# An attention, expert and gated-layer kernel: gated weights prepared ahead and kept in DRAM

## The chip, the cores and the metric

The program runs on one core of a Trainium2 chip. The metric is the device time of one execution, in microseconds (us). TensorE (PE in the profile) multiplies matrices, PEld is its weight load; VectorE is DVE, ScalarE is ACT, GpSimd is POOL; all DMAs here are issued by SyncE (SP).

## The reference

Three layers follow each other. An attention over 2 batches, 8 heads, 576 positions, width 64, where half of the heads see a local window of 32 positions and half see every 32nd position. Its output, 1152 tokens of width 512, goes through 4 experts that all work on all tokens, and then through a gated layer:

```
for e in range(E):                      # E = 4, F = 1024
    h = np.maximum(x @ w1[e], 0.0)
    out += p[:, e:e + 1] * (h @ w2[e])
...
gate = 1.0 / (1.0 + np.exp(-(x @ w_gate)))   # 512 -> 1536
val = x @ w_val
return (gate * val @ w_out).astype(np.float32)
```

The three weights of the gated layer come as float64 words, the others as float32.

## The kernel before, in words

**Number format.** TensorE gets most operands as pairs of float16, a high half and a low half (the rest after the high half), and each product takes three matmuls: high by high, high by low, low by high (`split_products`, L691 to L693). Before a weight can be used it must be prepared: read, its largest magnitude found on all partitions (`scale_on_chip`, with a small matmul, L261), scaled, and split. A gated weight is first turned from float64 words into float32 (`float32_of`, L428 to L435): each of its four chunks takes one ScalarE and four VectorE instructions.

**Seven products.** `x @ w_gate` and `x @ w_val` are done as 2 by 2 blocks with seven block products in place of eight (`seven`, L775 for the matmuls). For that each gated weight is prepared as seven block matrices, `W_B11` to `W_T4`, some of them sums and differences of blocks (L485 to L499), and the experts' output likewise (`x2_seven`, L327). Partial results are collected in four PSUM tiles b1 to b4, of which b1, b3 and b4 are accumulated into a second time, after ScalarE has copied b1 and b3 out (L800).

**Units.** The work is an ordered list of units. A unit is one layer half for one of three token blocks T of 384 tokens: `early_up` and `early_down` (expert 0, in float32), `expert_up` and `expert_down` (experts 1 to 3), `gated_up` (14 block products for one third j of the gated width) and `gated_down`. An up unit is followed by the down unit of the unit before it, so the gated part runs `gated_up(0,0)`, `expert_down(3,2)`, `gated_up(0,1)`, `gated_down(0,0)`, `gated_up(0,2)` and so on.

**Preparation in the gaps.** All engines run their instructions in program order, written out by hand (`manual_schedule`). Preparation is a generator for each item (15 items: 4 early, 6 expert, 6 gated `wg`/`wv` and 3 `wo`), cut into steps. When a unit's PSUM tile is complete, it yields "evac", and at that place the program inserts some steps ahead of the evacuation:

```
STEPS = dict(early_up=2, early_down=2, expert_up=2, expert_down=4, gated_up=2, gated_down=3)
...
if free_after[i] >= n:
    return
```

An item is begun only when its weight tiles are free (`free_after`, from the last unit that uses the tile's former content). There are nine such tiles: four in each of the slots wh and wl, and one more, wx. An expert item takes 24 steps, and a unit of each kind gives 16 (an `expert_up` has 8 evacuations of two steps, an `expert_down` 4 of four). A raw weight passes through four buffers, filled by SP (L158). Steps of an item that depend on each other on different engines are often issued one right behind the other: `put` in `prep_double` (L476) issues a ScalarE copy and a GpSimd subtraction that waits for it, and `gate` and `value` in `gated_up` issue a GpSimd or VectorE operation and a ScalarE operation that waits for it (L846 to L849, L861 to L867).

Of the kernel before, what the change touches and what calls it, by code (L numbers as in the profile page):

```python
# [36 lines left out]
STEPS = dict(early_up=2, early_down=2, expert_up=2, expert_down=4, gated_up=2, gated_down=3)  # L37
# [7 lines left out]
def attn_moe_glu_kernel(ctx, tc, q, k, v, dp, w1, w2, wg, wv, wo, out):  # L45
# [19 lines left out]
    pd = drp.tile([NTB * E, 128], F32, tag="pd", name="pd")  # L65
    gp = ctx.enter_context(tc.tile_pool(name="gp", bufs=PSUM_BUFS, space=PSUM))
# [53 lines left out]
    def add_item(kind, key, parts):  # L120
        i = len(items)
        items.append((kind, key))
        first_raw[i] = len(raw_list)
        for u, (src_, m) in enumerate(parts):
            raw_list.append((i, u, m, src_))

    for s in range(EARLY):
# [15 lines left out]
    item_of = {key: i for i, (_, key) in enumerate(items)}  # L143
    n_parts = dict(early=2, expert=2, seven=2, out=1)
# [112 lines left out]
    def scale_on_chip(col, m, top_to=TOP):  # L257

        ps = g_tile()
# [51 lines left out]
    X7, x2_done = {}, set()  # L311

# [14 lines left out]
    def x2_seven(T):  # L327
# [25 lines left out]
        put(X_A11, a11)  # L353
        yield
        put(X_A22, a22)
# [7 lines left out]
        put(X_S2, a22)  # L363
        yield
        nc.vector.tensor_tensor(a21, a11, a21, ALU.subtract)
        yield
        put(X_S3, a21)
        yield
        put(X_A12, a12)
# [3 lines left out]
        put(X_S4, a22)  # L373
# [64 lines left out]
    def prep_double(i):  # L438
# [3 lines left out]
        fs = []  # L442
        for u in range(4):
# [11 lines left out]
        sc = tmp["up"][:, i:i + 1]  # L455
        if items[i][0] == "out":
            t = w_tile(i, 0, [128, 2, 4, 512], F16, "w16")
            W16[i, 0] = t
            for c in range(4):
                f = fs[c // 2][:, c % 2, :]  # L460
                nc.scalar.activation(t[:, 0, c, :], f, AF.Copy, scale=sc)
                nc.scalar.activation(f, f, AF.Copy, scale=sc)
                nc.gpsimd.tensor_tensor(t[:, 1, c, :], f, t[:, 0, c, :], ALU.subtract)
                yield
            return
        for c in range(4):
            f = fs[c // 2][:, c % 2, :]
            nc.scalar.activation(f, f, AF.Copy, scale=sc)  # L468
            if c % 2:
                yield  # L470
        homes = [w_tile(i, x, [128, m, 2, 2, 256], F16, "w7") for x, m in ((0, 4), (1, 3))]
        W7[i] = lambda k: homes[k // 4][:, k % 4]
# [8 lines left out]
        put(W_B22, b22)  # L481
        yield
        put(W_B11, b11)
        yield
        nc.vector.tensor_tensor(b22, b22, b12, ALU.subtract)  # L485
        yield
        put(W_T3, b22)
        yield
        nc.vector.tensor_tensor(b12, b12, b11, ALU.subtract)
        yield  # L490
        put(W_T1, b12)
# [10 lines left out]
        yield  # L502
# [596 lines left out]
```

## Time and profile before

| what | us |
|---|---|
| median of 3 runs | 776.84 |
| lowest and highest | 771.44, 792.42 |
| the profiled execution, its own time | 772.87 |
| span of the profiled execution (first to last instruction) | 771.1 |
| PE busy, VectorE busy, ScalarE busy, GpSimd busy | 689.6, 442.1, 364.5, 259.6 |

Durations and waits below come from the one profiled execution. Busy times of PE overlap at their ends, since matmuls are pipelined: successive matmuls start closer together than one lasts. The granted clock (PEclk) is the share of full speed that TensorE was given in a stretch; full speed is 2.4 GHz, and the lower level is 1.2 GHz.

### The profile page before, as it was taken

Reading aid. Unit: us, or ns where it says so; the run is one execution under the profiler, and the core shown is the slowest. Engines: PE = TensorE matmul, PEld = TensorE weight load, DVE = VectorE, ACT = ScalarE, POOL = GpSimd, SP = SyncE. Lnnn points to the kernel's source line nnn. Section 1 sums busy time; section 2 is a strip of 40 time slices with the busy share of each in tenths; the row PEclk is TensorE's granted clock in tenths of the full one; section 3 lists DMA queues with packets and bytes.
Section 4 is the critical chain, followed back from the end, with each engine's and each line's share of the span. In section 5 each row is a group of like instructions: output and inputs, shape, how many; then the busy total and the mean of one; then the engine's idle time right before and its main releaser. Section 6 shows DMA issues by size and latency. Waiting matters only on the chain.

```text
span 771.1 us, 12481 instructions
## 1 busy us (share of the span) xinstructions
PE 689.6 (89%) x4886; PEld 506.9 (66%) x4887; DVE 442.1 (57%) x869; ACT 364.5 (47%) x884; POOL 259.6 (34%) x272
## 2 busy tenths in 40 slices
PE   8999999998999999999999986968756767768998
PEld 5778899995766666666666665665546455546884
DVE  3776656675444422426474667766758647584433
ACT  4666533545666454343543534436454653535220
POOL 2443430002223032131732432314642544445332
PEclk8979999999999999999999997979777978788999
DMA  9824140012232120303020000102113211100012
GB/s 190 196 76 107 56 129 33 1 56 92 93 110 93 53 95 11 110 21 101 1 82 28 1 28 28 56 28 82 55 55 110 63 48 55 56 0 2 1 42 83
DMA packets 38947, 48.68 MB, mean 63 GB/s; under 512 B 18436, under 2 KB 23336, under 8 KB 38888
## 3 DMA queue, kind: packets, MB, share of 16 engines
q1 hardware_dynamic: 38888, 47.89, 21.2%
q8 instruction: 38, 0.62, 0.3%
q14 instruction: 21, 0.17, 0.1%
HBM read 45.50 MB, written 2.38 MB: 62 GB/s over the span
## 4 chain that ended last, share of the span: by engine, by line
PE 63%; DVE 16%; ACT 8%; POOL 7%; issue 4%; DMA 2%; SPq 0%; POOLq 0%; DVEq 0%; ACTq 0%
PE gps L691 17%; PE gps L692 17%; PE gps L693 17%; PE gps L775 4%; POOL w L479 4%; DVE bits L433 2%; DVE bits L431 2%; DVE magn L435 2%; PE sps L562 1%; PE sps L575 1%; PE tps L605 1%; PE o L626 1%; ACT magn L468 1%; ACT sg L849 1%; DVE bits L429 1%
## 5 line engine op out<-in xcount | busy, mean ns | idle before, releaser
L775 PE MATMUL gps<-x,w 128*128 128x192 f16 x1512 | 155.8, 270 | 57.8 <-ACT four L800 54.5
L775 PEld LDWEIGHTS <-w 128*128 128x128 f16 x1512 | 144.8, 108 | 67.0 <-issue 62.2
L745 POOL TENSOR_TENSOR hl<-t,hh 128x384 f16<-128x384 f32 x72 | 69.3, 963 | 234.2 <-ACT t L744 234.2
L691 PE MATMUL gps<-hh,w 128*128 128x384 f16 x288 | 94.3, 327 | 0.0
L692 PE MATMUL gps<-hl,w 128*128 128x384 f16 x288 | 94.2, 327 | 0.0
L693 PE MATMUL gps<-hh,w 128*128 128x384 f16 x288 | 94.1, 327 | 0.0
L691 PE MATMUL gps<-x,w 128*128 128x384 f16 x288 | 93.9, 326 | 0.0
L692 PE MATMUL gps<-x,w 128*128 128x384 f16 x288 | 93.9, 326 | 0.0
L693 PE MATMUL gps<-x,w 128*128 128x384 f16 x288 | 93.9, 326 | 0.0
L691 PEld LDWEIGHTS <-w 128*128 128x128 f16 x576 | 56.5, 98 | 37.5 <-issue 0.5
L693 PEld LDWEIGHTS <-w 128*128 128x128 f16 x576 | 56.5, 98 | 37.4 <-issue 0.3
L692 PEld LDWEIGHTS <-w 128*128 128x128 f16 x576 | 56.5, 98 | 36.6 <-issue 0.2
L479 POOL TENSOR_TENSOR w<-magn,w 128x512 f16<-128x512 f32 x42 | 52.5, 1268 | 61.6 <-ACT w L478 61.6
L743 ACT ACTIVATE hh<-gps 128x384 f16<-128x384 f32 x72 | 35.2, 489 | 75.8 <-PE gps L693 75.7
L419 DVE SCALAR_TENSOR_TENSOR w<-raw,up,w 128x512 f16<-128x512 f32 x48 | 39.7, 833 | 29.1 <-ACT w L417 29.1
L589 ACT ACTIVATE P<-sps,nm 72x72 f32<-72x72 f32 (+1 forms) x112 | 36.4, 331 | 34.6 <-DVE nm L587 20.1
L763 DVE SCALAR_TENSOR_TENSOR t<-gps,comb,pb 128x384 f32<-128x384 f32 x36 | 22.1, 615 | 52.2 <-PE gps L693 50.4
L598 POOL TENSOR_TENSOR P<-P,sm 72x288 f32<-72x288 f32 (+1 forms) x32 | 27.0, 844 | 57.4 <-DVE sm L597 33.6
L866 ACT CAST hh<-gv 128x384 f16<-128x384 f32 x36 | 17.3, 508 | 60.7 <-POOL gv L861 55.1
L435 DVE SCALAR_TENSOR_TENSOR magn<-magn,bits 128x512 f32<-128x512 f32 x36 | 30.8, 856 | 25.1 <-ACT magn L428 22.5
L867 POOL TENSOR_TENSOR hl<-gv,hh 128x384 f16<-128x384 f32 x36 | 37.4, 1052 | 16.3 <-ACT hh L866 16.2
L691 PE MATMUL gps<-w,hh 128*128 128x512 f16 (+1 forms) x112 | 42.7, 382 | 0.0
(152 smaller groups left out, 1367.3 us busy)
## 6 DMA issues: line engine op xcount, KB each, us to landing
raw<-in_moe_w_dram SPq DMA_DIRECT2D x32, 512.0 KB
raw<-in_moe_w_gate_dram SPq DMA_DIRECT2D x12, 512.0 KB
raw<-in_moe_w_val_dram SPq DMA_DIRECT2D x12, 512.0 KB
raw<-in_moe_w_out_dram SPq DMA_DIRECT2D x12, 512.0 KB
pb<-pd SPq DMA_DIRECT2D x11, 192.0 KB
out_dram<-outacc SPq DMA_DIRECT2D x8, 256.0 KB
vl<-in_v_dram SPq DMA_DIRECT2D x8, 160.0 KB
vs<-in_v_dram SPq DMA_DIRECT2D x4, 288.0 KB
```

The source lines that it names most:

```text
L419: nc.vector.scalar_tensor_tensor(lo_, r[:, x], sc, hi_, ALU.mult, ALU.subtract)
L435: nc.vector.scalar_tensor_tensor(f, f, LEAST, a.bitcast(F32), ALU.is_ge, ALU.mult)
L479: nc.gpsimd.tensor_tensor(d[:, 1], s_, d[:, 0], ALU.subtract)
L589: nc.scalar.activation(pp[:, j, :], pv_[:, j, :], AF.Exp, bias=nm[:n, j:j + 1], accum_out=sm[:n, j:j + 1])
L598: nc.gpsimd.tensor_tensor(pp, pp, sm.unsqueeze(2).to_broadcast([n, m, w]), ALU.mult)
L691: nc.tensor.matmul(ps, ah, bh, start=i == 0, stop=False)
L692: nc.tensor.matmul(ps, ah, bl, start=False, stop=False)
L693: nc.tensor.matmul(ps, al, bh, start=False, stop=i == n - 1)
L743: nc.scalar.activation(dh, ps, AF.Relu, scale=DOWN)
L745: nc.gpsimd.tensor_tensor(dl, t, dh, ALU.subtract)
L775: nc.tensor.matmul(o, l_, r_, start=first and x + kk + y == 0, stop=last and x * kk * y == 2, skip_group_check=True)
L867: nc.gpsimd.tensor_tensor(dl, tv, dh, ALU.subtract)
```

## The change

Gated weights are no longer prepared into weight tiles but into small staging tiles (four buffers) and stored to DRAM as float16 pairs, one store of 256 KB for each of the 7 (or 4) matrices of an item; `load_parked` brings a whole item back by one or two DMAs when its weight tiles are free. So the preparation of gated items is not tied to weight tiles. The extra tile wx is gone. Steps are no longer inserted at evacuations but one for each `TICK` (0.9 us) of nominal TensorE time (`STEP_US` for each yield of a unit), `TICK_X2` (0.65 us) while the experts' output is being split. The items of the last expert are prepared behind wg and wv of j = 0. Within an item the ScalarE, GpSimd and VectorE steps of one matrix are set some steps apart, three of seven low halves go to VectorE, and two more pauses stand ahead of the small matmul of `scale_on_chip`. In `gated_up` the sigmoid and the split of a result are put off by some evacuations (`after`, `one_on`). The seven products come in another order, and T4 goes into b2 alone and not on top of T3 in b4.

```diff
-STEPS = dict(early_up=2, early_down=2, expert_up=2, expert_down=4, gated_up=2, gated_down=3)
+STEP_US = dict(early_up=0.53, early_down=0.53, expert_up=0.49, expert_down=0.49, gated_up=0.25, gated_down=0.65)
+TICK = 0.9
+TICK_X2 = 0.65
+PARK_BUFS = 4
...
+    parked = {}
+    for j in range(F2 // 512):
+        for name in ("wg", "wv", "wo"):
+            parked[name, j] = drp.tile([128, 4 if name == "wo" else 7, 1024], F16, tag=f"{name}{j}", name=f"{name}{j}")
...
+    prep_order = [i for i in range(NI) if items[i][1] not in (("w1", E - 1), ("w2", E - 1))]
+    at = prep_order.index(item_of["wo", 0])
+    prep_order[at:at] = [item_of["w1", E - 1], item_of["w2", E - 1]]
+    for i in prep_order:
+        first_raw[i] = len(raw_list)
+        for u, (src_, m) in enumerate(parts_of[i]):
+            raw_list.append((i, u, m, src_))
...
     def scale_on_chip(col, m, top_to=TOP):
 
+        yield "hold"
+        yield "hold"
         ps = g_tile()
...
+    put_off = []
+
+    def after(n, work):
+        put_off.append([n, work])
+
+    def one_on():
+        for p_ in put_off:
+            p_[0] -= 1
+        for p_ in [p_ for p_ in put_off if p_[0] < 0]:
+            put_off.remove(p_)
+            p_[1]()
...
-        def put(k, s_):
-            d = X7[T](k)
-            nc.scalar.activation(d[:, 0], s_, AF.Copy, scale=sc)
-            nc.vector.scalar_tensor_tensor(d[:, 1], s_, sc, d[:, 0], ALU.mult, ALU.subtract)
...
+        def high(k, s_):
+            nc.scalar.activation(X7[T](k)[:, 0], s_, AF.Copy, scale=sc)
+
+        def low(k, s_):
+            nc.vector.scalar_tensor_tensor(X7[T](k)[:, 1], s_, sc, X7[T](k)[:, 0], ALU.mult, ALU.subtract)
+
+        high(X_A11, a11)
+        high(X_A22, a22)
+        yield
+        low(X_A22, a22)
+        high(X_A12, a12)
         yield
         nc.vector.tensor_tensor(a22, a21, a22, ALU.add)
-        yield
-        put(X_S1, a22)
-        yield
+        high(X_S1, a22)
+        low(X_A11, a11)
+        yield
+        low(X_S1, a22)
         nc.vector.tensor_tensor(a22, a22, a11, ALU.subtract)
         yield
...
+        high(X_S4, a22)
+        low(X_S3, a21)
+        yield
+        low(X_S4, a22)
         yield
...
     def w_tile(i, part, shape, dt, name):
-        pool, tag = pool_of[i][part]
-        return (tmp["w"] if pool == "w2" else wp).tile(shape, dt, tag=tag, name=name)
+        return wp.tile(shape, dt, tag=pool_of[i][part][1], name=name)
...
+        measure = None
         for u in range(4):
             r = raw.pop((i, u))
             if u % 2 == 0:
                 fs.append(tmp["p"].tile([128, 2, 512], F32, tag="magn", name="magn", bufs=3))
             f = fs[-1][:, u % 2, :]
-            yield from float32_of(r, f)
+            for y, _ in enumerate(float32_of(r, f)):
+                if y == 1 and measure:
+                    magnitudes(*measure)
+                yield
             load_raw_to(n + u + 1 + RAW_BUFS)
-            magnitudes(pk[:, u:u + 1], f)
-            yield
+            measure = pk[:, u:u + 1], f
+        yield
+        magnitudes(*measure)
+        yield "hold"
         nc.vector.tensor_reduce(pk[:, 4:5], pk[:, :4], AX.X, ALU.max)
         yield "hold"
         yield from scale_on_chip(i, pk[:, 4:5], TOP_S if items[i][0] == "seven" else TOP)
         sc = tmp["up"][:, i:i + 1]
...
+        def high(k, s_, f):
+            d = tmp["p"].tile([128, 2, 512], F16, tag="stage", name="stage", bufs=PARK_BUFS)
+            view = lambda t: t.rearrange("p (a b) -> p a b", a=s_.shape[1]) if len(s_.shape) == 3 else t
+            nc.scalar.activation(view(d[:, 0]), s_, AF.Copy, scale=sc if f else 1.0)
+            if f:
+                nc.scalar.activation(s_, s_, AF.Copy, scale=sc)
+            halves_of[k] = d, view, s_
+
+        def low(k, eng):
+            d, view, s_ = halves_of.pop(k)
+            eng.tensor_tensor(view(d[:, 1]), s_, view(d[:, 0]), ALU.subtract)
+            nc.sync.dma_start(home[:, k, :], d.rearrange("p z f -> p (z f)"))
+
         if items[i][0] == "out":
-            t = w_tile(i, 0, [128, 2, 4, 512], F16, "w16")
-            W16[i, 0] = t
             for c in range(4):
-                f = fs[c // 2][:, c % 2, :]
-                nc.scalar.activation(t[:, 0, c, :], f, AF.Copy, scale=sc)
-                nc.scalar.activation(f, f, AF.Copy, scale=sc)
-                nc.gpsimd.tensor_tensor(t[:, 1, c, :], f, t[:, 0, c, :], ALU.subtract)
+                high(c, fs[c // 2][:, c % 2, :], True)
                 yield
+                if c:
+                    low(c - 1, nc.gpsimd)
...
-        for c in range(4):
-            f = fs[c // 2][:, c % 2, :]
...
-        def put(k, s_):
-            d = W7[i](k)
-            nc.scalar.copy(d[:, 0], s_)
-            nc.gpsimd.tensor_tensor(d[:, 1], s_, d[:, 0], ALU.subtract)
...
+        high(W_B22, b22, True)
+        yield
+        low(W_B22, nc.gpsimd)
+        high(W_B11, b11, True)
+        yield
+        nc.scalar.activation(b12, b12, AF.Copy, scale=sc)
+        low(W_B11, nc.vector)
+        yield
+        high(W_B21, b21, True)
+        yield
+        low(W_B21, nc.gpsimd)
+        sub(b22, b22, b12)
+        yield
+        high(W_T3, b22, False)
+        sub(b12, b12, b11)
+        yield
+        low(W_T3, nc.gpsimd)
+        high(W_T1, b12, False)
         yield
         nc.vector.tensor_tensor(b11, b22, b11, ALU.add)
         yield
-        put(W_T2, b11)
-        yield
-        put(W_B21, b21)
-        yield
-        nc.vector.tensor_tensor(b21, b21, b11, ALU.subtract)
-        yield
-        put(W_T4, b21)
-        yield
+        low(W_T1, nc.gpsimd)
+        high(W_T2, b11, False)
+        yield
+        low(W_T2, nc.vector)
+        yield
+        sub(b21, b21, b11)
+        yield
+        high(W_T4, b21, False)
+        yield
+        low(W_T4, nc.vector)
+        yield
+
+    def load_parked(i):
+
+        home = parked[items[i][1]]
+        if items[i][0] == "out":
+            t = w_tile(i, 0, [128, 4, 2, 512], F16, "w16")
+            nc.sync.dma_start(t.rearrange("p c z f -> p c (z f)"), home)
+            W16[i, 0] = t.rearrange("p c z f -> p z c f")
+            return
+        homes = []
+        for x, (m0, m1) in ((0, (0, 4)), (1, (4, 7))):
+            homes.append(w_tile(i, x, [128, m1 - m0, 2, 2, 256], F16, "w7"))
+            nc.sync.dma_start(homes[x].rearrange("p m z k f -> p m (z k f)"), home[:, m0:m1])
+        W7[i] = lambda k: homes[k // 4][:, k % 4]
 
...
         copied(p1, b1)
+        b3 = g_tile()[:, :TC]
+        yield from seven_product(b3, W(W_T1), X(X_S1), True, False)
+        yield "evac"
+        copied(p5, b3)
         b2 = g_tile()[:, :TC]
         yield from seven_product(b2, W(W_T2), X(X_S2), True, True)
         yield "evac"
         ready(u2, b2, p1)
-        b3 = g_tile()[:, :TC]
-        yield from seven_product(b3, W(W_T1), X(X_S1), True, False)
-        yield "evac"
-        copied(p5, b3)
         b4 = g_tile()[:, :TC]
-        yield from seven_product(b4, W(W_T3), X(X_S3), True, False)
+        yield from seven_product(b4, W(W_T3), X(X_S3), True, True)
         yield "evac"
         ready(v, b4, u2)
         done("22", None, (v, p5))
@@ -823,9 +889,9 @@
         yield from seven_product(b3, W(W_B22), X(X_S4), False, True)
         yield "evac"
         done("12", b3, u2)
-        yield from seven_product(b4, W(W_T4), X(X_A22), False, True)
+        yield from seven_product(b2, W(W_T4), X(X_A22), True, True)
         yield "evac"
-        done("21", b4, u2)
+        done("21", b2, v)
...
-                nc.gpsimd.tensor_tensor(sg[name], *other, ALU.add)
+                nc.gpsimd.tensor_tensor(t, *other, ALU.add)
             else:
-                nc.vector.tensor_tensor(sg[name], ps, other, ALU.add)
-            nc.scalar.activation(sg[name], sg[name], AF.Sigmoid, scale=cg)
+                nc.vector.tensor_tensor(t, ps, other, ALU.add)
+            after(2 if name == "22" else 1, lambda: nc.scalar.activation(t, t, AF.Sigmoid, scale=cg))
...
-            nc.scalar.copy(dh, tv)
-            nc.gpsimd.tensor_tensor(dl, tv, dh, ALU.subtract)
+
+            def split():
+                nc.scalar.copy(dh, tv)
+                nc.gpsimd.tensor_tensor(dl, tv, dh, ALU.subtract)
+
+            after({"11": 1, "12": 2, "21": 1, "22": 3}[name], split)
...
-    slots = {("w1", "wh"): [], ("w1", "wl"): [], ("w2", "wx"): []}
-    bufs_of = dict(w1=W_BUFS, w2=1)
+    slots = {("w1", "wh"): [], ("w1", "wl"): []}
...
-        occ, bufs = slots[slot], bufs_of[slot[0]]
-        if len(occ) >= bufs:
-            return last_use[occ[-bufs]]
-        return -1 if slot[0] == "w1" else N_EARLY
+        occ = slots[slot]
+        return last_use[occ[-W_BUFS]] if len(occ) >= W_BUFS else -1
...
-    todo = list(range(NI))
+    todo = list(prep_order)
     going = []
+    to_load = [i for i in range(NI) if items[i][0] in ("seven", "out")]
...
                 i = todo[0]
-                if free_after[i] >= n:
+                if items[i][0] in ("early", "expert") and free_after[i] >= n:
                     return
...
+    def load_some(n):
+        busy = set(todo) | {i for _, i in going}
+        if any(items[i][0] == "expert" for i in busy):
+            return
+        while to_load and to_load[0] not in busy and free_after[to_load[0]] < n:
+            load_parked(to_load.pop(0))
...
+        credit = 0.0
+
+        def background(n):
+            if gated:
+                split_x2(1)
+            elif (x16_next[0] < 2 or n > units.index(("early_up", EARLY - 1, x16_next[0] - 1))) and \
+                    next(halves, "end") != "end":
+                pass
+            else:
+                prep_some(n, 1)
...
             if u == ("gated_down", 0, 0):
+                while gated:
+                    split_x2(1)
...
-            rate = STEPS[u[0]]
+                load_some(n)
             for y in unit_steps(u):
-                if n < N_EARLY and y is None:
-                    n_none += ATT_RATE
-                    while n_none >= 1:
-                        attend()
-                        n_none -= 1
-                if y == "evac":
-                    if n >= N_EARLY:
-
-                        if gated:
-                            split_x2(2)
-                            continue
-                        if x16_next[0] < 2 or n > units.index(("early_up", EARLY - 1, x16_next[0] - 1)):
-                            if next(halves, "end") != "end":
-                                prep_some(n, 1)
-                                continue
-                    prep_some(n, rate)
+                if n < N_EARLY:
+                    if y is None:
+                        n_none += ATT_RATE
+                        while n_none >= 1:
+                            attend()
+                            n_none -= 1
+                    if y == "evac":
+                        prep_some(n, 2)
+                elif y == "evac":
+                    one_on()
+                elif y is None:
+                    credit += STEP_US[u[0]]
+                    while credit >= (TICK_X2 if gated else TICK):
+                        credit -= TICK_X2 if gated else TICK
+                        background(n)
```

## Rows read from the trace of the kernel before

**Rows 1.** Page, section 2: busy tenths of TensorE in 40 slices of the span.

```profile
PE   8999999998999999999999986968756767768998
```

**Rows 2.** Windows: length; busy us of PE, PEld, DVE, ACT, POOL; PEclk; DMA share; GB/s.

```profile
186.00:452.70 266.70, 266.70 (x1644) 163.98 (x1643) 123.09 (x215) 129.29 (x264) 84.23 (x85) 1.00 0.19 60
452.70:706.00 253.30, 182.66 (x1439) 143.37 (x1437) 174.45 (x301) 127.69 (x254) 103.14 (x89) 0.82 0.16 51
706.00:771.10 65.10, 60.97 (x516) 44.83 (x515) 26.34 (x46) 14.38 (x30) 23.51 (x25) 0.99 0.10 38
```

**Rows 3.** Timeline of PE, gated part: start us, length us, instruction, count.

```profile
452.74 3.13 PE L775 MATMUL gps<-x,w 128*128 128x192 f16 x36
...
716.52 14.02 PE L775 MATMUL gps<-x,w 128*128 128x192 f16 x168
...
738.15 14.02 PE L775 MATMUL gps<-x,w 128*128 128x192 f16 x168
...
767.48 0.27 PE L693 MATMUL gps<-w,hl 128*128 128x256 f16 x1
```

**Rows 4.** Waits of PE, 452.7 to 706 us: waiter, releaser, total us, times, longest.

```profile
PE gps L775 <- ACT four L800: 52.5, 19, 8.3
PE gps L261 <- DVE gpk L452: 10.1, 5, 3.9
```

**Rows 5.** Waits of ScalarE and VectorE, 452.7 to 706 us.

```profile
ACT hh L866 <- POOL gv L861: 37.6, 12, 5.9
...
DVE magn L499 <- POOL w L479: 19.9, 4, 6.4
```

**Rows 6.** Groups of VectorE, 452.7 to 706 us: count, busy us, mean ns, idle before.

```profile
L431 DVE SCALAR_TENSOR_TENSOR bits<-raw,bits 128x512 uint32<-128x512 uint32 x28 | 24.5, 875 | 0.6
L433 DVE SCALAR_TENSOR_TENSOR bits<-raw,bits 128x512 uint32<-128x512 uint32 x28 | 24.0, 858 | 0.8
L435 DVE SCALAR_TENSOR_TENSOR magn<-magn,bits 128x512 f32<-128x512 f32 x28 | 23.6, 844 | 9.7 <-ACT magn L428 7.6
L429 DVE TENSOR_SCALAR bits<-raw 128x512 uint32<-128x512 uint32 x28 | 15.7, 562 | 0.3
L351 DVE SCALAR_TENSOR_TENSOR x<-x2acc,up,x 128x384 f16<-128x384 f32 x14 | 8.5, 618 | 12.0 <-ACT x L350 12.0
L795 DVE TENSOR_TENSOR four<-gps,four 128x384 f32<-128x384 f32 x14 | 7.7, 551 | 0.7 <-PE gps L775 0.7
...
L485 DVE TENSOR_TENSOR magn<-magn 128x512 f32<-128x512 f32 x4 | 6.5, 1628 | 16.9 <-POOL w L479 16.9
...
L895 DVE SCALAR_TENSOR_TENSOR outacc<-gps,cv,outacc 128x512 f32<-128x512 f32 x6 | 4.5, 743 | 0.0
...
L332 DVE TENSOR_REDUCE x2pk<-x2acc 128x1 f32<-128x768 f32 x4 | 3.6, 940 | 0.0
...
L878 DVE TENSOR_TENSOR cv<-cv,down 128x1 f32<-128x1 f32 x5 | 3.0, 593 | 0.2
...
L499 DVE TENSOR_TENSOR magn<-magn 128x512 f32<-128x512 f32 x4 | 2.8, 693 | 19.9 <-POOL w L479 19.9
```

**Rows 7.** Windows of 20 us in which VectorE was busiest.

```profile
580.00:600.00 20.00, 15.26 (x131) 13.38 (x131) 18.29 (x34) 10.13 (x23) 5.04 (x5) 0.76 0.34 107
...
640.00:660.00 20.00, 13.35 (x98) 9.79 (x97) 18.54 (x31) 7.87 (x18) 6.98 (x7) 0.77 0.28 95
```

**Rows 8.** ScalarE, 186 to 452.7 us, one group: count, busy us, mean ns, idle before.

```profile
L743 ACT ACTIVATE hh<-gps 128x384 f16<-128x384 f32 x69 | 33.8, 490 | 75.8 <-PE gps L693 75.7
```

**Rows 9.** The 20 us window of the expert units with the most ScalarE work.

```profile
360.00:380.00 20.00, 20.00 (x126) 12.05 (x125) 7.88 (x14) 13.05 (x28) 12.71 (x12) 1.00 0.09 28
```

**Rows 10.** Timeline of PE ahead of the first expert weights.

```profile
184.59 0.23 PE L261 MATMUL gps<-identb,wpk 128*128 128x128 bf16 x1 [2.85 <-DVE wpk L407]
```

**Rows 11.** A 20 us window with much DMA traffic.

```profile
100.00:120.00 20.00, 20.00 (x134) 19.23 (x133) 10.84 (x23) 4.25 (x9) 5.22 (x5) 1.00 0.40 123
```

**Rows 12.** Waits of SP: the last store, 128 KB.

```profile
SPq L1095 <- DMA out_dram<-outacc: 1.4, 1, 1.4
```

More of the change, by code (lines that the diff above doesn't have):

```diff
@@ L122, in add_item @@
         items.append((kind, key))
-        first_raw[i] = len(raw_list)
-        for u, (src_, m) in enumerate(parts):
-            raw_list.append((i, u, m, src_))
+        parts_of[i] = parts
+    parts_of = {}
     for s in range(EARLY):
@@ L346, in x2_seven @@
         a21, a22 = a[:, 0:2, hc:TC], a[:, 2:4, hc:TC]
-        def put(k, s_):
-            d = X7[T](k)
-            nc.scalar.activation(d[:, 0], s_, AF.Copy, scale=sc)
-            nc.vector.scalar_tensor_tensor(d[:, 1], s_, sc, d[:, 0], ALU.mult, ALU.subtract)
-        put(X_A11, a11)
+        def high(k, s_):
[4 more added lines that the diff above has]
+        high(X_A22, a22)
         yield
-        put(X_A22, a22)
+        low(X_A22, a22)
+        high(X_A12, a12)
         yield
         nc.vector.tensor_tensor(a22, a21, a22, ALU.add)
+        high(X_S1, a22)
+        low(X_A11, a11)
         yield
-        put(X_S1, a22)
-        yield
+        low(X_S1, a22)
         nc.vector.tensor_tensor(a22, a22, a11, ALU.subtract)
         yield
-        put(X_S2, a22)
-        yield
+        high(X_S2, a22)
         nc.vector.tensor_tensor(a21, a11, a21, ALU.subtract)
         yield
-        put(X_S3, a21)
+        high(X_S3, a21)
+        low(X_A12, a12)
         yield
-        put(X_A12, a12)
+        low(X_S2, a22)
         yield
@@ L464, in prep_double @@
                 yield
-            return
-        for c in range(4):
-            f = fs[c // 2][:, c % 2, :]
-            nc.scalar.activation(f, f, AF.Copy, scale=sc)
-            if c % 2:
-                yield
-        homes = [w_tile(i, x, [128, m, 2, 2, 256], F16, "w7") for x, m in ((0, 4), (1, 3))]
-        W7[i] = lambda k: homes[k // 4][:, k % 4]
+                if c:
+                    low(c - 1, nc.gpsimd)
+                    yield
+            low(3, nc.gpsimd)
+            yield
@@ L473, in prep_double @@
+            return
         b11, b12 = fs[0][:, :, 0:256], fs[0][:, :, 256:512]
         b21, b22 = fs[1][:, :, 0:256], fs[1][:, :, 256:512]
-        def put(k, s_):
-            d = W7[i](k)
-            nc.scalar.copy(d[:, 0], s_)
-            nc.gpsimd.tensor_tensor(d[:, 1], s_, d[:, 0], ALU.subtract)
-        put(W_B22, b22)
+        sub = lambda o, x, y: nc.vector.tensor_tensor(o, x, y, ALU.subtract)
+        high(W_B22, b22, True)
         yield
-        put(W_B11, b11)
+        low(W_B22, nc.gpsimd)
@@ L494, in prep_double @@
         yield
-        put(W_T2, b11)
+        low(W_T1, nc.gpsimd)
+        high(W_T2, b11, False)
         yield
-        put(W_B21, b21)
+        low(W_T2, nc.vector)
         yield
-        nc.vector.tensor_tensor(b21, b21, b11, ALU.subtract)
+        sub(b21, b21, b11)
         yield
-        put(W_T4, b21)
+        high(W_T4, b21, False)
         yield
+        low(W_T4, nc.vector)
+        yield
+    def load_parked(i):
+        home = parked[items[i][1]]
+        if items[i][0] == "out":
[8 more added lines that the diff above has]
+        W7[i] = lambda k: homes[k // 4][:, k % 4]
     def prep_weights(i):
@@ L841, in gate @@
             sg[name] = tmp["p"].tile([128, TC], F32, tag="pb", name="sg", bufs=PB_BUFS)
+            t = sg[name]
             if name == "11":
[L843 removed]
+                nc.scalar.activation(t, ps, AF.Sigmoid, scale=cg)
                 return
             if name == "22":
[L846 removed]
+                nc.gpsimd.tensor_tensor(t, *other, ALU.add)
             else:
[L848 to L849 removed]
+                nc.vector.tensor_tensor(t, ps, other, ALU.add)
+            after(2 if name == "22" else 1, lambda: nc.scalar.activation(t, t, AF.Sigmoid, scale=cg))
         def value(name, ps, other):
@@ L962, in load_p_some @@
             p_next[0] += 1
-    todo = list(range(NI))
+    todo = list(prep_order)
     going = []
+    to_load = [i for i in range(NI) if items[i][0] in ("seven", "out")]
     def waiting():
-        return set(todo) | {i for _, i in going}
+        return set(todo) | {i for _, i in going} | set(to_load)
     def prep_some(n, steps=2):
```

9 lines of the change are left out of this document (2 added, 7 removed).

## The prediction

> **What bounds the kernel now.** I read the row of slices first: TensorE is busy in nine tenths or more of nearly every slice until a little past the middle, and then falls to six to eight tenths [rows 1]. The windows say where: in the expert units, 186 to 452.7 us, TensorE is busy all the time at full clock, and VectorE and ScalarE less than half of it; in the gated units up to 706 us it is busy 182.66 of 253.30 us at a granted clock of 0.82; in the last 65 us, when no preparation is left, it is back at 61 us and 0.99 [rows 2]. So the loss lies in the gated units while they prepare weights, and no other engine is full there: VectorE, the busiest, has 174.45 of 253.3 us, 0.69.
>
> What would these units take without the loss? The timeline shows two `gated_up` in the quiet part, each 168 matmuls in a row in 14.02 us, begun 21.63 us apart [rows 3]; between them lies one `gated_down`. 14.02 counts the last matmul to its modelled end, which I put at 0.16; so 13.86 and 7.77 us. One `expert_down` is 96 matmuls of 266.70 / 1644 = 0.162 us [rows 2], 15.6 us. From the first gated matmul at 452.7 on there are nine of each gated unit and one `expert_down`: 9 x 21.63 + 15.6 = 210.3 us. The last matmul ended at 767.7 [rows 3], 315.0 us after. **The loss is 104.7 us**, and nothing done in the gated part can give more.
>
> Whom TensorE waits for: the copy of b1 and b3 by ScalarE, 52.5 us in 19 waits, and the largest-magnitude reduction ahead of the small matmul, 10.1 us [rows 4]. The copy is short; ScalarE reaches it late, since it stands still ahead of instructions that wait for others: 37.6 us for GpSimd's product in `value` [rows 5] (other pairs like it make up less each). VectorE in turn waits 19.9 us at L499 for a low half on GpSimd [rows 5]. The rest of the 104.7 is the lower clock that follows such gaps: 182.66 us of busy TensorE for work that takes 210.3 - 61 = 149 us at full speed.
>
> **The change, part by part.** *Moved preparation.* There are 36 float64 chunks (9 items of 4). In 452.7 to 706 us stand 28 of each of their four VectorE instructions [rows 6]; so only 8 were done among the experts, since items waited for weight tiles. After the change an item needs no tile. I count steps against ticks. A gated `wg`/`wv` item has 22 steps up to its scale and 13 behind, a `wo` 30, an expert item 24, the split of the attention output 33, the split of the experts' output 16 for each T. The eight early units that remain give 16 x 0.53 / 0.9 = 9.4 ticks each, an expert unit 32 x 0.49 / 0.9 = 17.4, a `gated_up` 56 x 0.25 / 0.9 = 15.6, a `gated_down` 8.7. Up to `gated_up(0,0)` that is 75 + 17 x 17.4 = 371 ticks, less some 12 in which the first experts' output is split; 33 go to the attention output, 144 to expert items, and 182 are left for gated items: five whole ones, and 13 steps of the sixth, `wo` of j = 1. In the gated part remain 13 chunks, the rest of that item, two `wg`/`wv` items and the last `wo`; by the same count they end in `gated_up(1,2)`, about 116 us in. No unit finds its item unprepared; the nearest are the first expert weights, some 8 ticks (7 us) ahead, though wx is gone.
>
> *Cover among the experts.* Before, those units took steps at 16 in 15.6 us whenever a tile was free, 0.98 us a step; now 0.9 and never blocked. The window with most ScalarE work has 13.05 of 20 us with TensorE full and clock 1.00 [rows 9]. Worst is an `expert_up` over the 13 steps that split a gated matrix: 16 evacuations of 0.490 [rows 8] and about 14 copies of the same kind in 15.6 us, over by some 2 us; the next `expert_down` evacuates on VectorE and gives it back, and eight PSUM tiles stand between. Five such units: 0 to +10 us, I take +2, nearer to the full windows.
>
> *What is late next in the gated part: VectorE.* Its work over the first 116 us (five `gated_up`, four `gated_down`, the `expert_down`: 5 x 21.63 - 7.77 + 15.6 = 116.0 at full clock), by [rows 6]: 13 chunks of 0.875 + 0.858 + 0.844 + 0.562 = 3.14, 40.8; two splits of the experts' output, 2 x (2 x 0.940 + 7 x 0.618 + 4 x 0.551) = 16.8; behind the scale of two items four sums, L485 and L499 the ends of them, mean 1.16, and three low halves newly on VectorE, priced as L435 at 0.844, 2 x (4.6 + 2.5) = 14.2; five `gated_up` of nine operations as L795 and one as L435, 29.0; the `expert_down`'s eight as L351, 4.9; three L895, 2.2; and small ones, of which eight groups, the largest 3.0, came to 14 us in all, some 8. **Sum 116 us of VectorE in 116 us of TensorE.** If it never idled, this would cost 0. If it stayed at the 0.69 it had, 116 / 0.69 = 168, +52. In its two densest windows it had 18.29 and 18.54 of 20 [rows 7], 0.92: 126, +10. There its queue was always full; an even pace leaves it no stock of work, and some of its steps still wait for halves from ScalarE and GpSimd. I take 0.87: 133, **+17**, nearer to the dense windows because the pairs that held it stand apart now.
>
> *Waits taken apart.* Sigmoids and splits are put off by one to four evacuations, about 1 us each, where GpSimd needs one operation; W_B21 into b1 comes as late as before, but b3 is copied one product earlier, and T4 no longer needs b4 read. This is why I let the 52.5 us go. The two further pauses give the reduction 2.7 us in place of 0.9; its waits up to 3.9 us [rows 4] shrink but stay where VectorE lags, inside the +17. The wait of 2.85 us ahead of the first expert scale [rows 10] goes: -2.8 (bounds -2.9 and 0).
>
> *Stores and loads.* The change adds 54 stores of 256 KB, 14.2 MB, and as much of loads, on SP. SP computes nothing; behind a store that waits for its low half are queued raw loads, which stand three to four chunks (11 to 14 us) ahead, and behind a load that waits for a tile the same. DMA moved 123 GB/s at a share of 0.40 [rows 11], some 307 GB/s when busy; a whole `wv` of 1.83 MB takes 6.0 us. The tightest are `wv` of j = 1 and of j = 2: begun a `gated_down` and half a `gated_up` before their use, 14.7 us. A store holds ScalarE only if its staging buffer is wanted again, four matrices or some 5 us later; 256 KB are 0.85 us, and the last store of 128 KB kept SP 1.4 us [rows 12]. So 0, with a rival for late loads. The Trainium skill speaks against such transfers (DMA: Bandwidth & Descriptors, Bandwidth and Rules for kernel authors): it wants a MiB or more in each, and lists 1 MB at 6.15 us. No row here has a single large load; by that page the estimate for 1.83 MB is some 11 us, still under 14.7, and the sum would be the same.
>
> **Sum.** Against the execution's own 772.9: -104.7, +17, +2, -2.8 gives 684.4. That execution stands 4.0 below the median of the runs, 776.84; I add 1.6 for it: **686 us**.
>
> **Rivals.**
> - *VectorE stays as stuck as it was* (0.69): in place of +17, +52. 772.9 - 104.7 + 52 + 2 - 2.8 = 719. For it: its 116 us in 116; against: half of its longest waits are for pairs now parted. 0.11.
> - *The change doesn't do what it says about waits:* ScalarE still reaches the copies late, and the loss falls only as the preparation left does, to 104.7 x 13/28 = 48.6 us: 772.9 - 104.7 + 48.6 - 2.8 = 714. 0.11.
> - *Loads late:* the loads at the end of `gated_up(0,2)` (`wv`, `wo` of j = 1, then `wg` of j = 2, 4.7 MB or 15 us) hold up raw chunks or `wv`; four late ones of 6 us, on top of the sum: about 708. 0.08.
> - *Slower than before:* stores land late. If each of the 54 keeps its staging buffer past the 5 us until it is wanted, ScalarE stands still at the next high half, and the evacuations behind it. The gain of 88 us is gone from 1.7 us exposed for each store; at 2.2 us it is 684 + 119 = 803. For it: loads of 1 to 1.8 MB share the queue; against: [rows 12] and a DMA share of 0.16 [rows 2]. 0.05.
> - *Forecast*, TensorE nearly full with VectorE next: 665 to 704. 0.65.
>
> **Range and chances.** With no loss at all it is 772.9 - 104.7 - 2.8 = 665; the two rivals at 714 and 719 belong inside: 664 to 718; outside lie the slower case and tails on both sides. A measurement of this kernel can tell about 2% from no change, 761 to 792: faster 0.93, same 0.03, slower 0.04.
>
> **What the new profile would show.** Right: about 22 to 24 of 36 chunks before the first L775; TensorE full among the experts; from the first L775 to the last matmul 225 to 230 us, VectorE near 0.87 in the first half of that, then windows of full TensorE; waits of L775 for L800 under 10 us. Wrong: TensorE waiting for ScalarE with ScalarE waiting for DMA at the staging tiles (slower), PE waiting for DMA of w7 tiles (late loads), gaps and clock below 1 among the experts (the +2 is mis-sized), L800 still ahead of the waits.

## The result, and the profile after

| | before | after |
|---|---|---|
| median, lowest to highest (4 runs each) | 784.63, 771.44 to 792.84 | 702.18, 701.11 to 702.58 |
| profiled execution, own time and span | 772.87, 771.1 | 701.11, 699.3 |
| first gated matmul to the end of the last matmul | 315.0 | 228.2 |

The ratio is 0.9068, 95% interval 0.9011 to 0.9125. Executions of both kernels come in two groups, 16 to 20 us apart, by TensorE's clock in the attention: the ratio sets the lower group of before (771 to 777) against runs after that are all in the upper one; upper against upper, 702.2 to about 792.6, it is 0.886.

The page after, section 2, answers to [rows 1]: busy tenths of TensorE and granted clock in 40 slices.

```profile
PE   8999999999999999999999999998899899899998
...
PEclk8555799999999999999999999999999999999999
```

The fall behind the middle is gone. What is new is a clock of 5 in the second to fourth slices. Windows after, cut where units begin, columns as in [rows 2]:

```profile
0.00:75.40 75.40, 73.13 (x458) 55.10 (x459) 33.97 (x114) 34.59 (x170) 24.15 (x46) 0.59 0.53 118
75.40:192.90 117.50, 117.50 (x791) 109.94 (x790) 81.24 (x188) 56.21 (x162) 22.83 (x29) 0.99 0.24 71
192.90:468.00 275.10, 274.42 (x1691) 168.24 (x1691) 192.65 (x312) 166.59 (x340) 98.89 (x92) 1.00 0.41 131
468.00:584.00 116.00, 108.05 (x967) 86.73 (x965) 96.76 (x170) 69.30 (x135) 54.03 (x44) 0.96 0.41 141
...
468.00:601.00 133.00, 125.05 (x1115) 99.49 (x1113) 112.71 (x197) 78.04 (x155) 61.71 (x50) 0.96 0.38 129
```

The third stretch begins with the first expert matmul, some 10 us ahead of that of [rows 2]. VectorE has 192.65 of 275.1 us among the experts, where before it had 123.09 of 266.7 [rows 2], or 127.53 of 277.0 from the first expert matmul on, and TensorE is still full there. The ends of the gated part, timeline after, as in [rows 3]:

```profile
468.02 3.88 PE L841 MATMUL gps<-x,w 128*128 128x192 f16 x45
...
695.94 0.27 PE L759 MATMUL gps<-w,hl 128*128 128x256 f16 x1
```

Waits of TensorE after, gated part, as in [rows 4] (L866 is the copy, L276 the small matmul), and of ScalarE, as in [rows 5]:

```profile
PE gps L276 <- DVE x2pk L361: 4.1, 2, 2.1
PE gps L841 <- ACT four L866: 3.0, 4, 1.3
PE gps L276 <- DVE gpk L490: 2.4, 2, 2.1
PE gps L841 <- DVE four L861: 0.8, 1, 0.8
...
ACT junk L292 <- DVE magn L467: 26.9, 14, 4.6
...
ACT hh L935 <- POOL gv L928: 9.2, 10, 1.9
```

The 52.5 us of waits for the copies are 3.0, ScalarE's wait for GpSimd 37.6 is 9.2, and no wait for a DMA stands among TensorE's. The longest of ScalarE is now the one for VectorE ahead of the magnitudes, 26.9 us, hardly less than before (29.2). Where the time is more than forecast is seen in the attention, whose instructions the change leaves alone. Windows of before:

```profile
20.00:40.00 20.00, 19.74 (x214) 15.94 (x212) 14.71 (x52) 14.10 (x73) 10.86 (x18) 0.93 0.80 184
40.00:60.00 20.00, 19.03 (x149) 15.26 (x145) 14.37 (x46) 13.25 (x68) 8.90 (x14) 0.67 0.25 77
```

and of after:

```profile
20.00:40.00 20.00, 20.00 (x135) 16.18 (x134) 8.46 (x28) 9.51 (x50) 6.21 (x10) 0.50 0.78 176
40.00:60.00 20.00, 20.00 (x116) 15.28 (x114) 9.26 (x32) 8.75 (x42) 7.82 (x11) 0.50 0.22 55
60.00:80.00 20.00, 20.00 (x132) 16.82 (x132) 11.75 (x39) 10.41 (x50) 6.26 (x11) 0.54 0.28 69
```

TensorE is busy all the time at half its clock and does 251 matmuls in 40 us, where before it did 363. The first early unit begins at 59.2 us before and at 75.5 after: 16.3 us.

### The profile page after: what moved, and what is told of

Its sections match the earlier page's. It is cut to its first block, busy times and chain, and to the rows that moved or that the text cites. A ratio compares the mean times of both kernels' runs of the same rounds, so it can differ in the third digit from the quotient of the medians.

```text
span 699.3 us, 12745 instructions
## 1 busy us (share of the span) xinstructions
PE 682.8 (98%) x4887; PEld 504.7 (72%) x4887; DVE 463.1 (66%) x887; ACT 366.1 (52%) x884; POOL 245.4 (35%) x254
## 2 busy tenths in 40 slices
DMA packets 48885, 77.01 MB, mean 110 GB/s; under 512 B 19540, under 2 KB 24440, under 8 KB 47672
## 4 chain that ended last, share of the span: by engine, by line
PE 73%; DVE 16%; ACT 5%; issue 3%; DMA 3%; SPq 0%; POOL 0%; DVEq 0%; ACTq 0%; POOLq 0%
PE gps L757 17%; PE gps L759 17%; PE gps L758 17%; PE gps L841 9%; PE sps L641 3%; PE tps L671 2%; DVE bits L463 2%; PE o L692 2%; PE sps L628 2%; DVE bits L465 2%; DVE magn L467 1%; DVE bits L461 1%; DVE x L378 1%; DVE magn L522 1%; DMA ks<-in_k_dram 1%
## 5 line engine op out<-in xcount | busy, mean ns | idle before, releaser
L811 POOL TENSOR_TENSOR hl<-t,hh 128x384 f16<-128x384 f32 x72 | 73.8, 1029 | 192.5 <-ACT t L810 192.3
L841 PE MATMUL gps<-x,w 128*128 128x192 f16 x1512 | 132.9, 251 | 3.9 <-ACT four L866 3.0
L841 PEld LDWEIGHTS <-w 128*128 128x128 f16 x1512 | 129.4, 100 | 7.5 <-issue 4.9
L759 PEld LDWEIGHTS <-w 128*128 128x128 f16 x576 | 56.3, 98 | 37.3
L757 PEld LDWEIGHTS <-w 128*128 128x128 f16 x576 | 56.3, 98 | 37.2 <-issue 0.3
L758 PEld LDWEIGHTS <-w 128*128 128x128 f16 x576 | 56.3, 98 | 36.4
L507 POOL TENSOR_TENSOR stage<-magn,stage 128x512 f16<-128x512 f32 x36 | 46.6, 1305 | 51.2 <-ACT magn L502 49.0
L292 ACT ACTIVATE junk<-magn 128x512 bf16<-128x512 f32 x36 | 22.7, 630 | 60.2 <-DVE magn L467 60.2
L451 DVE SCALAR_TENSOR_TENSOR w<-raw,up,w 128x512 f16<-128x512 f32 x48 | 38.1, 811 | 20.5 <-ACT w L449 20.5
L809 ACT ACTIVATE hh<-gps 128x384 f16<-128x384 f32 x72 | 34.9, 485 | 29.2 <-PE gps L759 29.1
L757 PE MATMUL gps<-w,hh 128*128 128x512 f16 (+1 forms) x112 | 41.6, 372 | 0.0
L758 PE MATMUL gps<-w,hh 128*128 128x512 f16 (+1 forms) x112 | 41.6, 372 | 0.0
L759 PE MATMUL gps<-w,hl 128*128 128x512 f16 (+1 forms) x112 | 41.6, 372 | 0.0
```

Source lines behind the costliest of these rows:

```text
L292: nc.scalar.activation(junk[:, :n], x.rearrange("p a b -> p (a b)") if len(x.shape) == 3 else x, AF.Abs, accum_out=col)
L451: nc.vector.scalar_tensor_tensor(lo_, r[:, x], sc, hi_, ALU.mult, ALU.subtract)
L507: eng.tensor_tensor(view(d[:, 1]), s_, view(d[:, 0]), ALU.subtract)
L757: nc.tensor.matmul(ps, ah, bh, start=i == 0, stop=False)
L758: nc.tensor.matmul(ps, ah, bl, start=False, stop=False)
L759: nc.tensor.matmul(ps, al, bh, start=False, stop=i == n - 1)
```

## The experiments

Each had a profile and timed runs beside the kernel before: four, but ten for "before, again", six for "after, again" and seven for "before, warm". "Warm" means 16 more warm-up matmuls; the variants below "after, tied" are "after, warm" with one more edit each. The number of a line shifts a little from variant to variant. "Early and experts" goes from the first early unit to the first gated matmul, "gated" from there to the end of the last matmul, of the profiled execution.

| kernel | median (range) | first early unit | early and experts | gated |
|---|---|---|---|---|
| before | see above | 59.2 | 393.5 | 315.0 |
| after | see above | 75.5 | 392.5 | 228.2 |
| before, again | 773.26 (768.07 to 792.77) | 54.9 | 396.3 | 315.0 |
| after, again | 701.36 (686.01 to 702.84) | 76.4 | 393.3 | 228.2 |
| before, warm | 777.50 (774.32 to 779.32) | 63.0 | 396.1 | 314.8 |
| after, warm | 689.09 (686.11 to 689.10) | 61.7 | 392.0 | 227.5 |
| after, tied | 731.75 (731.65 to 732.44) | 58.9 | 392.0 | 276.0 |
| warm, nothing put off | 699.41 (698.69 to 699.98) | 63.7 | 392.5 | 238.3 |
| warm, old order | 687.81 (681.11 to 691.47) | 64.6 | 393.2 | 228.7 |
| warm, light VectorE | 675.88 (675.29 to 677.59) | 61.8 | 392.6 | 216.8 |
| warm, step each 0.8 us | 703.82 (701.75 to 707.14) | 61.7 | 408.6 | 226.5 |
| warm, step each 0.7 us | 732.09 (730.58 to 734.07) | 61.6 | 431.6 | 234.0 |
| warm, stored twice | 689.03 (685.24 to 695.10) | 62.3 | 394.4 | 228.6 |
| warm, old steps | 715.00 (708.17 to 715.67) | 61.4 | 393.5 | 254.9 |

**The start: both kernels again.** 

> The kernel before, unchanged, so that each execution's granted clock is seen. In the changed kernel's profile the first early unit starts at 75.4 us, against 59.1 before, at a granted clock of 0.50 from 15 to 70 us; the instructions up to there are the same. Theory A (the slow start is a state that an execution of either kernel falls into): the runs of this kernel fall into two groups some 16 to 20 us apart, about 772 to 777 with a mean clock near 0.93 and about 792 with a lower one. Theory B (the changed program brings the slow start): all runs stay within a few us of 772 to 777 here, and what lay at 792 had another cause, with no drop of the mean clock.

Three of its ten executions lie at 791.3 to 792.8 with a mean clock of 0.900 to 0.902, seven at 768.1 to 776.9 with 0.922 to 0.933. Of 49 executions of before on all occasions 20 lie over 790 and 29 under 778. Theory A holds, B falls. No execution of before near 792 was profiled: that its time is lost in the attention is inferred from the mean clock, and from the warm-up below. Nor are all below 778 alike in the attention: the one profiled here starts its first early unit at 54.9, and shows the lower clock only behind 40 us.

```profile
20.00:40.00 20.00, 19.73 (x220) 15.52 (x215) 15.87 (x54) 15.48 (x78) 12.30 (x20) 1.00 0.99 227
40.00:60.00 20.00, 19.03 (x128) 15.98 (x126) 12.09 (x40) 10.70 (x52) 7.01 (x11) 0.57 0.35 82
```

> The changed kernel, unchanged, in more executions. If the slow start is a state that each execution falls into by chance, as the kernel before does in about half of its executions, there is a second group near 682 to 687 with a mean clock near 0.97; if the changed program always falls into it, all lie at 700 to 703 with a clock near 0.946.

Five of six at 700.6 to 702.8 with a clock of 0.944 to 0.951, one at 686.01 with 0.973. So the changed kernel too has both, but of its ten executions nine have the lower clock.

**Warming up.**

```diff
             if i < 5:
                 keep_warm(2)
+            if i in (4, 9):
+                keep_warm(8)
```

> The changed kernel with 16 more warm-up matmuls of 512 columns in the attention, 8 in its fifth and 8 in its tenth step. They cost 3.4 us at full clock and 6.8 us at the lower one. Theory A (a slow start by TensorE's clock is all that the forecast missed): the clock is back at 1.0 by some 30 us, the first early unit starts 9 to 13 us earlier than 75.4, the time is 688 to 694. Rival (the attention is slow for another reason, and the clock only follows): the start stays at 75 or later, and the time is 702 to 709.

> The kernel before with the same 16 warm-up matmuls. Theory A: its runs no longer fall into two groups; all lie near 772 to 780, the first early unit starts at 59 to 63 us. Theory B: nothing but the cost of the matmuls, +3 to +7 us on each group.

Theory A held for both: before stays at 774 to 779 in all 7 executions (ratio to the lower group 1.0064, 1.0035 to 1.0092) and starts its first early unit at 63.0, after is at 686 to 689 in all four. Windows of the changed kernel with it:

```profile
20.00:40.00 20.00, 19.94 (x198) 14.45 (x198) 12.28 (x40) 11.93 (x61) 8.76 (x14) 0.95 0.77 184
40.00:60.00 20.00, 19.03 (x164) 14.93 (x163) 15.13 (x50) 13.70 (x67) 9.85 (x14) 0.73 0.27 74
```

The two bursts cost more than nothing, but the first early unit begins 13.8 us earlier, just more than the 9 to 13 expected. The clock is back by 22 us; the lower one from 40 to 60 us (0.73) is there as in before (0.67). Because this kernel's start is steadier, all variants but the tied one carry it: their profiles start the first early unit at 61.4 to 64.6. Their times still spread by up to 10 us, so small differences are read from the gated part of one profile each.

**Items tied to weight tiles again**, in the old order of items.

```diff
...
+    prep_order = list(range(NI))
...
-                if items[i][0] in ("early", "expert") and free_after[i] >= n:
+                if free_after[i] >= n:
```

> The changed kernel in which a gated item is again begun only when its weight tiles are free, in the old order of items; staging, stores, loads, the even pace, the parted waits and the new order of the products stay. Theory (moving the preparation ahead is most of the gain): of the 36 chunks fewer than 12 come ahead of the first gated matmul, the gated part takes 270 us or more in place of 228, and the time is over 740. Rival (the parted waits and the even pace are most of it): the gated part takes under 250 us, the time is below 725.

24 of 36 chunks lie in the gated part, which takes 276.0 us: of the 86.8 gained, 39.0 come with pace, parted waits and order alone, and 47.8 with the preparation moved ahead. The tied kernel also stores and loads its weights, without the ninth tile, so the 47.8 holds against this variant and not against preparation straight into tiles. The theory's bound of 270 held, its share ("most") only just; 12 chunks came ahead where it had fewer than 12; the time is under its 740, because the attention began the early unit at 58.9, with no warm-up added. Waits of TensorE in the gated part:

```profile
PE gps L274 <- DVE gpk L488: 27.5, 2, 16.3
PE gps L839 <- ACT four L864: 17.9, 6, 7.1
PE gps L755 <- DMA w<-wo: 4.6, 2, 4.2
```

The first is the price of late items: TensorE stands at the small matmul, up to 16.3 us at a time, until VectorE has the item's largest magnitude. In the third a load comes late.

**Nothing put off.**

```diff
-        put_off.append([n, work])
+        work()
```

> The changed kernel with the 16 warm-up matmuls, and with nothing put off: each sigmoid and each split is issued right behind what it waits for, as before. Compared with the same kernel with the warm-up matmuls alone (689.1, gated part from the first gated matmul to the last matmul 227.5). Theory (parting the waits matters): ScalarE again waits for GpSimd's product, TensorE for the copies of b1 and b3, 15 us or more, and the gated part takes 238 or more. Rival (an even pace alone keeps ScalarE free): the gated part stays within 3 us.

The theory held: the gated part is 10.8 us longer. ScalarE waits for GpSimd again, and TensorE for ScalarE, 15.3 us against 6.9 in "after, warm":

```profile
ACT hh L937 <- POOL gv L930: 58.0, 18, 4.3
ACT sg L918 <- POOL sg L915: 26.2, 9, 4.8
...
PE gps L843 <- ACT four L868: 15.3, 10, 4.7
```

**Old order of the products** (T2 ahead of T1, T4 accumulated on T3 in b4).

```diff
...
-        yield from seven_product(b2, W(W_T4), X(X_A22), True, True)
+        yield from seven_product(b4, W(W_T4), X(X_A22), False, True)
```

> The changed kernel with the 16 warm-up matmuls and the old order of the seven products (T2 ahead of T1, T4 on top of T3 in b4). Theory: the copy of b3 comes one product later, so TensorE waits a little more for it, 2 to 8 us over the 18 passes: gated part 230 to 236. Rival (the order is without effect): within 2 us.

The rival held: 1.2 us in one profile, times from 681 to 691, on both sides of 689. An effect of the order isn't shown.

**Light VectorE.**

```diff
-        nc.vector.scalar_tensor_tensor(a, hi_, 0xC0000000, a, ALU.bitwise_and, ALU.bitwise_or)
         yield
-        nc.vector.scalar_tensor_tensor(a, lo_, 29, a, ALU.logical_shift_right, ALU.bitwise_or)
         yield
```

> The changed kernel with the 16 warm-up matmuls, leaving out two of the four VectorE instructions that turn a float64 chunk into float32 (the sign and the low bits are dropped); the steps stay, empty. In the gated part that takes 13 x 1.73 = 22 us from VectorE. Theory (VectorE is what is late in the gated part, the forecast's +17): the gated part falls from 227.5 to 212 to 219, close to the 210.3 that TensorE needs. Rival (the loss sits in dependences, not in VectorE's load): it falls by less than 4 us.

216.8 us, 10.7 less, within the theory's range. Waits of TensorE in the gated part of "after, warm", and of the light variant:

```profile
PE gps L843 <- ACT four L868: 6.9, 9, 1.7
PE gps L276 <- DVE x2pk L361: 4.1, 2, 2.1
PE gps L276 <- DVE gpk L490: 2.5, 2, 2.1
...
PE gps L841 <- ACT four L866: 4.0, 4, 1.6
PE gps L276 <- DVE x2pk L361: 0.6, 1, 0.6
```

So 10.7 of the 17.2 us by which the gated part stays above 210.3 go with these instructions of VectorE: 6.6 us of waits ahead of the small matmul fall to 0.6, 6.9 at the copies to 4.0. The two instructions are also links in the chain from a chunk to its scale; the wait for x2pk, which is no part of that chain, fell most, and that speaks for the load.

**Other paces.** `TICK = 0.8` and `TICK = 0.7`.

> The changed kernel with the 16 warm-up matmuls and one step in 0.8 us of TensorE time in place of 0.9 (the split of the experts' output stays at 0.65). Some 45 more steps come ahead of the gated part, so 8 chunks in place of 13 are left there, 16 us less for VectorE. Theory (VectorE is what is late in the gated part, and the experts have room): the gated part falls from 227.5 to 217 to 222, the stretch of the experts (first expert matmul to first gated matmul, 275.3) grows by 0 to 3, the time is 680 to 686 against 689.1. Rival (the experts are full at this pace): their stretch grows by 8 or more, the time is 689 or more.

> As before, with one step in 0.7 us. VectorE would have some 0.85 to 0.9 of the experts' stretch and ScalarE, in an expert_up, more than the stretch. Theory: what the gated part gains (to 213 to 219) is mostly lost among the experts (+5 to +15): time 680 to 692. Rival (PSUM tiles and the next expert_down absorb it all): experts' stretch within 3 us of 275.3, time 674 to 680.

Both theories fell. At 0.8 the rival's numbers came (the experts' stretch is 10.5 us longer, 285.8, the time 703.8), but not for its reason, as the loads below show; at 0.7 the stretch is 35 us longer, beyond both. At 0.8 VectorE has 87.08 us in the first 116 us of the gated part, 10.5 less than with 0.9 (97.56), and yet that part is only 1.0 us shorter; ahead of it 16.6 us are lost. Windows at 0.8 (early, experts) and TensorE's longest waits in the two together:

```profile
61.70:184.50 122.80, 118.42 (x791) 110.55 (x789) 85.16 (x196) 59.59 (x168) 22.88 (x29) 0.98 0.24 70
184.50:470.30 285.80, 277.60 (x1693) 168.41 (x1693) 202.56 (x338) 176.49 (x366) 106.94 (x97) 0.99 0.44 142
...
PE gps L276 <- DVE gpk L490: 7.3, 5, 2.5
PE gps L276 <- DVE wpk L439: 4.7, 3, 3.9
```

VectorE has 0.71 and ScalarE 0.62 of the experts' stretch: neither is full. TensorE stands ahead of the small matmul of `scale_on_chip`, 12.0 us in these two lines, where "after, warm" has 0.8. The reason that I see is that its pauses are counted in steps, so a quicker pace makes them shorter, and the chain of magnitudes and reduction is no quicker. At 0.7 the waits for gpk among the experts are 18.6 us. That longer pauses would save the quicker pace was not tried, so this reason is argued and not shown; nor was a pace slower than 0.9 tried.

**Stores twice.**

```diff
...
             nc.sync.dma_start(home[:, k, :], d.rearrange("p z f -> p (z f)"))
+            nc.sync.dma_start(spare[items[i][1]][:, k, :], d.rearrange("p z f -> p (z f)"))
```

> The changed kernel with the 16 warm-up matmuls in which each of the 54 staging tiles is stored twice, the second time to a DRAM tile that nothing reads: 14.2 MB more traffic, a staging buffer held about twice as long. The forecast took stores and loads at nothing. If that is right with room to spare: within 1% of 689.1 and no wait of ScalarE for a DMA. If the stores are near their limit: ScalarE waits for staging tiles, TensorE for late loads, 700 or more.

No difference in time can be seen (689.03, 685 to 695, against 689.09), 1.1 us in the gated part. With 91.17 MB in place of 77.01 TensorE still waits for no DMA of these tiles. ScalarE does, at the staging tiles, against the expectation: once in the changed kernel (first line), five times or 9.1 us here.

```profile
ACT stage L500 <- DMA wg<-stage: 4.5, 1, 4.5
...
ACT stage L503 <- DMA wg1s<-stage: 6.2, 2, 6.0
...
ACT stage L503 <- DMA wv0s<-stage: 2.6, 2, 2.3
...
ACT stage L503 <- DMA wg0s<-stage: 0.3, 1, 0.3
```

All of these lie among the experts, where TensorE's one longer wait, for gpk, grows from 0.8 to 2.3 us and the stretch from 275.3 to 277.2. So the rival's mechanism is there, but costs at most some 2 us where it was feared to cost 11 or more.

**Old steps at evacuations.**

```diff
-                    credit += STEP_US[u[0]]
...
+                    for _ in range(STEPS[u[0]]):
+                        background(n)
```

> The changed kernel with the 16 warm-up matmuls, but with the old fixed numbers of steps at each evacuation (2, 4, 2, 3 and so on) in place of the even pace; staging, stores, parted waits stay. Among the experts it is 16 steps for a unit in place of 17.4, in a gated_up 28 in place of 15.6. Theory (the pace matters in the gated part, where VectorE is full): preparation bunches there, VectorE runs late, gated part 235 to 250, time 697 to 712. Rival (only the amount moved ahead matters): gated part 227 to 232.

254.9 us, 27.4 more and above the theory's 250: these steps cost more here than waits that aren't parted (10.8). Evenness alone is not isolated: a `gated_up` also has 28 steps in place of 15.6, and 17 chunks in place of 14 are left for the gated part. Waits of TensorE in it:

```profile
PE gps L844 <- ACT four L869: 13.1, 9, 3.6
PE gps L277 <- DVE x2pk L362: 6.5, 2, 6.2
PE gps L844 <- DVE four L866: 4.8, 5, 1.7
```

## Why the prediction was right, and where its sum was off

*The loss and its place.* 104.7 less 17 was to be gained in the gated part, 87.7; it was 86.8. The floor of 210.3 was a good measure: with light VectorE the gated part comes within 6.5 of it. One reading was loose: 182.66 us of busy TensorE for 149 us of work make 34 of the 42 us that the two named waits leave; the rest is smaller waits and not the clock.

*Moved preparation.* The count of steps left 13 chunks for the gated part; 14 stand there. No unit found its item unprepared.

*VectorE late next.* 116 us of its work were to take 133; in the first 133 us it was busy 112.7 (0.85 against 0.87). The size was right: the gated part stands 17.9 us above its floor in the changed kernel and 17.2 in "after, warm". So was most of the mechanism: the light variant takes back 10.7 of 17.2, more than half of it as TensorE's waits ahead of the small matmul. Of the 6.5 us that stay, 4.0 are waits for the copies. How the 17 splits differs between executions: in the changed kernel 10.3 us are waits, with a clock of 0.96 over the first 116 us; in "after, warm" 14.3 are waits, with a clock of 1.00. The pace of 0.8 shows that less work for VectorE doesn't help where the wait ahead of the small matmul grows.

*Experts +2 and first scale -2.8.* Together -0.8; the stretch became 1.0 us shorter, 393.5 to 392.5. The wait ahead of the first expert scale is gone. The "2 us" for an `expert_up` don't follow from the price named beside them: 30 operations of 0.490 us are 14.7, inside 15.6.

*Waits taken apart.* 52.5 us fell to 3.0 (6.9 in "after, warm"), and come back in part when nothing is put off. The order of the products, which I named as a reason beside it, has no effect that can be seen.

*Stores and loads at nothing.* Right for the time, with room for twice the stores; ScalarE waits once for a store, 4.5 us among the experts, where TensorE idles 0.7 us in all. The Trainium skill's rule of a MiB or more in each transfer (DMA: Bandwidth & Descriptors, Rules for kernel authors) did not bind at 256 KB: the stores lie beside TensorE's work, at a DMA share of 0.41 among the experts and in the first 116 us of the gated part.

*The term that was off* is the last of the sum: "That execution stands 4.0 below the median of the runs, 776.84; I add 1.6 for it". The executions don't scatter around a median; they are of two kinds, by the clock of the attention, and the profiled one was of the quicker. The sum of 684.4 is for that kind and is met by the one execution of after of that kind (686.01); nine of ten are of the other, 16 us longer. 771.44 and 792.42 in the runs shown could have told. That 702 still lies in the range is luck: its upper part was there for the rivals at 714 and 719, and no term was there for the attention. Why the changed kernel falls into it in nine of ten, and before in 20 of 49, with the same instructions up to there, stays open; the tied variant, without warm-up, had 731.7 to 732.4 in four of four, with an early start in the one profiled.

Of the rivals, waits that stay and loads that come late are refuted by the waits after, the stuck VectorE by its 0.85, the late stores by storing twice.

## What to carry to other kernels

Preparation that is tied to the place it ends in runs when that place is free, not when the engines are: a parking place in DRAM set it free here at no cost in time that can be seen, worth 47.8 us against the same kernel with tied items; the pace of the steps and the waits set apart on in-order engines go with the rest. Engine loads don't show what pace an order of work can bear: 0.9 us was the best of the three tried, and at 0.8 it was in-order TensorE that broke first, at an instruction that ends a chain whose pauses are counted in steps. Where executions of one kernel spread by over 2%, compare their granted clocks before you take a median: here 16 warm-up matmuls turn 702 into 689 (0.892 of the lower group of before, 0.887 to 0.897); no variant that does all of the work was clearly quicker.

## What the hardware showed

In the two profiles of the changed kernel without more warm-up TensorE stood at its lower clock (0.50) from about 13 to 78 us and from 12 to 80 us. From 15 to 75 us it was busy all the time, with no wait listed, in the small matmuls of the attention; it came back when the long matmuls of the early unit had begun (at 75.5 and 76.4 us). In the profile of before, with the same instructions, it came back at 23 us, and was lower again from 47 to 60 us, behind a wait of 0.97 us. 16 matmuls of 512 columns in two bursts did away with the long stretch each time they were tried: by their times in 11 executions of two kernels, and in the profiles of all seven variants that carry them. Two short stretches stay, about 12 to 22 and 49 to 63 us in "after, warm". What decides between the long and the short ones is open.
